# Attention and GELU layer on one core: V of batch 0 issued earlier, loads of batch 2 released earlier and totalled later

## The chip, the cores and the metric

The kernel runs on one core of one Trainium2 chip. The metric is the device time of one execution, in microseconds. The core has five engines that run their own instruction streams in order: TensorE (PE, with its weight loads as PEld), VectorE (DVE), ScalarE (ACT), GpSimd (POOL) and SyncE (SP). DMAs are issued from the queues of SyncE, ScalarE and GpSimd.

## The reference

Batch 8, 12 heads, 448 positions, head size 64. Normalised attention, then a GELU layer over all 3584 tokens:

```python
def rmsnorm(x, g):
    rms = np.sqrt(np.mean(x * x, axis=-1, keepdims=True) + 1e-06)
    return x / rms * g
q_n, k_n = (rmsnorm(q, g_q), rmsnorm(k, g_k))
scores = scale * np.matmul(q_n, k_n.transpose(0, 1, 3, 2))
scores = scores - np.max(scores, axis=-1, keepdims=True)
attn = np.exp(scores)
attn = attn / (np.sum(attn, axis=-1, keepdims=True) + 1e-09)
x = np.matmul(attn, v)            # then (batch, seq, heads * 64)
h = x @ w_in                      # 768 -> 2048
g = 0.5 * h * (1.0 + np.tanh(c * (h + 0.044715 * h * h * h)))
return (g @ w_out)                # 2048 -> 768
```

## The kernel before

**Tiling.** A batch has three groups c of four heads. For each group and each of q and k, one tile of 128 partitions by 896 float32 values is loaded (`load`, L106, 448 KB). It is squared (`square`, L139 on ScalarE, L141 on GpSimd), summed over each head's 64 values (`total`, L146, VectorE), turned into 1/rms (`rsqrt` on ScalarE, L171 to L190, or `rsqrt_newton` on VectorE for batch 1), scaled into bf16 (`normed`, L228) and transposed, either by TensorE (`trans`: `turn` L246, `put` L255 to L259) or by a DMA from SyncE (`dma_trans`, L269). After a DMA transpose `gain` (L275, VectorE) multiplies k by the two gains; it waits for the DMA.

**Attention.** A unit is a group c and one of seven blocks t of 64 keys: eight score matmuls (L288) and one exp on ScalarE (L292) into `ex`. `key_sums` (L308 to L314, VectorE) adds some blocks so that fewer matmuls are needed for the sums. `products(..., 0, ...)` multiplies `ex` with ones (the sums), `products(..., 1, ...)` with V (`vb`), both L336 into the same two PSUM tiles `oall`. So between the two `turned` (L345, VectorE) has to copy the sums away, and `quad_x` (L360, VectorE) has to read the V products before the next group's sums. `recips` is L351 and L352.

**Order.** The whole order is written out by hand (`manual_schedule`): each engine executes in the order in which the program calls it. `first_attention` runs batch 0's 21 units one by one with the lists `side` and `mid` hung on the units. Then for each batch b the loop runs the first matrix product of b (`mm1_pair` L433, `mm1` L369, GELU in L438 and L375) with the list `m1`, and `attention(b + 1, ...)`, which interleaves the second matrix product (`mm2`, L389, copied out by L412, stored by SyncE in L421). `attention` takes two units as a group, i = 0 to 10, and starts each group with the entries of `side` under that number; the sums of c = 0 and 1 stand in groups 4 and 8, their V products and `quad_x` in groups 5 and 9; those of c = 2 come after the last group.

**Loads and buffers.** The tiles of q and of k come from rings of four buffers each. Before any load is issued, buffers are handed out in the order in which the program frees earlier ones. At the start a fourth tile of each is taken and marked by VectorE (`held`, L557), and GpSimd frees it with `released` (L641) after its second w_out load. `late_loads` (L120) does a load after a memset of one element by VectorE, so that SyncE issues the load only when VectorE has come to that place; `loads` has no such memset. Squares that GpSimd makes for batch 2 go into two buffers (`sqp`), so a square waits for the total that reads the one two before it.

**The start.** q of batch 0, group 0 is loaded in two halves, k in a part of four blocks (`t_first`) and a rest of three (`t_rest`). SyncE issues the first of each, ScalarE the second; behind them SyncE issues groups 1 and 2. GpSimd's first instructions are two small loads of the gains (L73), the identity, the square of k's rest (L598), part of q's scaling, two small products (L610, L611), the squares of group 1, then V (`load_v`, L129), the squares of group 2, and the loads of w_in (L576, eight in all) and w_out (L579).

Of the kernel before, what the change touches and what calls it, by code (L numbers as in the profile page):

```python
# [17 lines left out]
def kernel(  # L18
# [11 lines left out]
    nc = tc.nc  # L30
# [11 lines left out]
    HP = H // 2  # L42
# [57 lines left out]
    def load(b, c, n, parts=1, engs=(nc.sync,)):  # L100
        t = rawqk.tile([P, 2, NT, D], F32, tag=f"raw{n}", name=f"raw{n}")
        src = {"q": q, "k": k}[n]
        raws[n, b, c] = t
        m = 2 // parts
        return [
            lambda i=i: engs[i].dma_start(  # L106
                t[:, i * m:(i + 1) * m].rearrange("p a t d -> p a (t d)"),
                src[b, 4 * c + 2 * i * m:4 * c + 2 * (i + 1) * m].rearrange(
                    "(a r) (p t) d -> (r p) a (t d)", r=2, t=NT
                ),  # L110
            )
            for i in range(parts)
        ]

    def loads(b, c):
        for n in "qk":
            for go in load(b, c, n):
                go()

    def late_loads(b, c):  # L120

        for n in "qk":
            for go in load(b, c, n):
                nc.vector.memset(raws[n, b, c][:1, 0, 0, :1], 0.0)
                go()

    def load_v(b, i, n):

        nc.gpsimd.dma_start(  # L129
            vb[b % 2][:, i:i + n].rearrange("p a t d -> p a (t d)"),  # L130
            v[b, 2 * i:2 * (i + n)].rearrange("(a r) (p t) d -> (r p) a (t d)", r=2, t=NT),
        )

    def square(b, c, n, eng, hs=both, ts=slice(0, NT)):
        if (n, b, c) not in sqs:
            sqs[n, b, c] = sqp.tile([P, 2, NT, D], F32, tag="sq", name="sq")
        sq, raw = sqs[n, b, c][:, hs, ts], raws[n, b, c][:, hs, ts]
        if eng is nc.scalar:
            nc.scalar.activation(sq, raw, AF.Square)  # L139
        else:  # L140
            eng.tensor_mul(sq, raw, raw)  # L141

    def total(b, c, n, hs=both, ts=slice(0, NT)):
        if b not in sss:
            sss[b] = smp.tile([P, NCH, 2, 2, NT], F32, tag="ss", name="ss")
        nc.vector.reduce_sum(  # L146
            sss[b][:, c, "qk".index(n), hs, ts], sqs[n, b, c][:, hs, ts], axis=AX.X
        )
# [44 lines left out]
    def rsqrt_newton(b):  # L193

        rinvs[b] = smp.tile([P, NCH, 2, 2, NT], F32, tag="rinv", name="rinv")
        flat = "p c n a t -> p (c n a t)"
        y, ms = rinvs[b].rearrange(flat), sss[b].rearrange(flat)
        t = smp.tile([P, NCH * 4 * NT], F32, tag="lg", name="lg")
        nc.vector.tensor_scalar(ms, ms, 1.0 / D, 1e-6, op0=ALU.mult, op1=ALU.add)
        nc.vector.tensor_scalar(  # L200
            y.bitcast(I32), ms.bitcast(I32), -0.5, float(0x5F3759DF), op0=ALU.mult, op1=ALU.add
        )
        for i in range(3):
            nc.vector.tensor_mul(t, y, y)
            nc.vector.scalar_tensor_tensor(t, t, -0.5, ms, op0=ALU.mult, op1=ALU.mult)
            if i < 2:
                nc.vector.scalar_tensor_tensor(y, t, 1.5, y, op0=ALU.add, op1=ALU.mult)
        m = 4 * NT
        for i, c in enumerate((1, 0, 2)):
            dst = y[:, c * m:(c + 1) * m]  # L210
            if c != 1:
                dst = place(b, c)
            nc.vector.scalar_tensor_tensor(  # L213
                dst, t[:, c * m:(c + 1) * m], 1.5, y[:, c * m:(c + 1) * m],
                op0=ALU.add, op1=ALU.mult,
            )

    def idle(n, w):

        for _ in range(n):  # L220
            nc.tensor.matmul(w, zeros[:, :128], zeros, start=True, stop=True)
# [39 lines left out]
    def trans(b, c):  # L261
        for n in "qk":
            turn(b, c, n)
            put(b, c, n)
# [9 lines left out]
    def gain(b, c):  # L274
        nc.vector.tensor_scalar(kT[:, c], kT[:, c], gcol[:, 0:1], None, op0=ALU.mult)  # L275
# [255 lines left out]
    def plan(*entries):  # L531
        steps = {}
        for slot, *fns in entries:
# [4 lines left out]
    t_first, t_rest = slice(0, 4), slice(4, NT)  # L538
    halves = load(0, 0, "q", 2, (nc.sync, nc.scalar))
    raws["k", 0, 0] = rawqk.tile([P, 2, NT, D], F32, tag="rawk", name="rawk")  # L540
    halves += [
        lambda ts=ts, eng=eng: eng.dma_start(
            raws["k", 0, 0][:, :, ts].rearrange("p a t d -> p a (t d)"),
            k[0, :4].rearrange("(a r) (p t) d -> r p a t d", r=2, t=NT)[:, :, :, ts]
            .rearrange("r p a t d -> (r p) a (t d)"),
        )
        for ts, eng in ((t_first, nc.sync), (t_rest, nc.scalar))
    ]
    for go in halves:
        go()  # L550
# [33 lines left out]
    def warm():  # L584
        return oall[0][:, :S]

    def gpsimd_waits(x):

        nc.gpsimd.tensor_copy(mark, x)  # L589
# [4 lines left out]

    q_only, k_only = slice(0, 1), slice(1, 2)

    idle(18, warm())
    square(0, 0, "k", nc.gpsimd, ts=t_rest)  # L598
    for a in range(2):
# [13 lines left out]
    nc.vector.transpose(gcols, gprod)  # L613
    square(0, 1, "q", nc.gpsimd)
    square(0, 1, "k", nc.gpsimd)
    load_v(0, 0, HP)
    square(0, 2, "q", nc.gpsimd)
    square(0, 2, "k", nc.gpsimd)
    w_in_part(0, 2)
# [19 lines left out]
    def released():  # L639
        for t in held:  # L640
            nc.gpsimd.memset(t[:1, 0, 0, :1], 0.0)  # L641

    side = [(1, lambda: loads(1, 0)),
            (7, lambda: loads(1, 1)),
            (14, lambda: loads(1, 2))]
# [38 lines left out]
    def transposed(b, c):  # L684
        for n in "qk":
            dma_trans(b, c, n)

    def squared(b, c, n, a):
        square(b, c, n, nc.scalar, slice(a, a + 1))

    def normed_both(b, c, eng):
        for n in "qk":
            normed(b, c, n, eng)

    m2 = []
    for b in range(B):
        m1, side = [], []
        if b == 0:

            m1 = [(0, lambda: total(1, 1, "q"),  # L700
                   lambda: total(1, 1, "k"), lambda: total(1, 2, "q"), lambda: total(1, 2, "k"),
                   lambda: rsqrt_newton(1), lambda: normed_both(1, 1, nc.gpsimd)),
                  (4, lambda: transposed(1, 1), lambda: normed_both(1, 0, nc.vector),
                   lambda: normed_both(1, 2, nc.vector)),
                  (5, lambda: trans(1, 0)),
                  (7, lambda: trans(1, 2))]
            side += [(2, lambda: gain(1, 1), lambda: late_loads(2, 0)),
                     (3, lambda: late_loads(2, 1), lambda: late_loads(2, 2))]
            for c, slots in ((0, (4, 5)), (1, (6, 7)), (2, (8, 9))):
                for n, slot in zip("qk", slots):  # L710
                    side += [(3, lambda c=c, n=n: square(2, c, n, nc.gpsimd)),
                             (slot, lambda c=c, n=n: total(2, c, n))]
        elif b + 1 < B:

            m1.append((0, lambda: gpsimd_waits(ess[b, NCH - 1][:1, 0, :1])))
            for c in range(NCH):
                m1 += [(0, lambda c=c: normed_both(b + 1, c, nc.gpsimd)),
                       (4 * c + 4, lambda c=c: transposed(b + 1, c))]
            m1 += [(9, lambda: gain(b + 1, 0)), (14, lambda: gain(b + 1, 1))]
            side.append((3, lambda: gain(b + 1, 2)))  # L720
        if 0 < b and b + 2 < B:
            m1 += [(4, lambda: loads(b + 2, 1)), (8, lambda: loads(b + 2, 2))]
            for c, at in ((0, 4), (1, 9)):
                for i, (n, a) in enumerate((n, a) for n in "qk" for a in range(2)):
                    m1.append((at + i, lambda c=c, n=n, a=a: squared(b + 2, c, n, a)))
                m1 += [(at + 2, lambda c=c: total(b + 2, c, "q")),
                       (at + 4, lambda c=c: total(b + 2, c, "k"))]
            for n in "qk":
                m1.append((13, lambda n=n: square(b + 2, 2, n, nc.gpsimd)))
                side.append((0, lambda n=n: total(b + 2, 2, n)))  # L730
        m1 = plan(*m1)
        for f in range(nf // 2 if b == 0 else nf):
            if b == 0:
                if f > 1:
                    mm1_pair(f)
            elif f in (1, 3):
                mm1_pair(f // 2, late, b)
            elif f > 3:
                mm1(b, f)
            for fn in m1.get(f, ()):  # L740
                fn()
        m2 += m2_parts(b)
        if b + 1 == B:
            for fn in m2:
                fn()
            break
        nc.scalar.preload_act_table_set(EXP_SET)  # L747
        if b + 2 < B:
            side += [(10, lambda: rsqrt(b + 2)),
                     (0 if b else 5, lambda: load_v(b + 2, 0, HP))]  # L750
            if b + 3 < B:
                side.append((1, lambda: loads(b + 3, 0)))
        attention(b + 1, m2, 96 if b == 0 else 112, plan(*side))


# [28 lines left out]
```

## Time and profile before

| | |
|---|---|
| Runs of the kernel before | median 424.75 us (423.63 to 426.59, 3 runs) |
| Profiled execution | 426.47 us, of which the span from first to last instruction is 424.7 us |
| Granted TensorE clock, mean | 0.996 |
| Bytes moved by DMA | 54.06 MB; read 45.61 MB, written 11.01 MB |
| First attention, last exp ends | 33.2 us |
| Attention of batch 1, first scores to first sums of group 2 | 55.5 to 88.5 us |
| Each batch from then on | 48.4 us |

A share of busy time is a mean over the whole span. What a stage is worth is read from the waits in that stage: a line of the timeline has its start, its busy time, engine, line, operation, `out<-in`, and in brackets the idle time of the engine ahead of it with what ended that. In the chain of waits each piece has start, length, and the engine or DMA. A line of the DMA view has the packets of a queue, its MB, and the time of those packets as a share of 16 DMA engines; q0 is GpSimd's queue, q1 SyncE's, q10 ScalarE's.

### The profile page before, as it was taken

To read this page: it belongs to the slowest core of one execution; us is meant where nothing else is said; L and a number is where in the kernel's file an instruction comes from. 1 tells how busy PE (TensorE), PEld (TensorE's weight loads), DVE (VectorE), ACT (ScalarE), POOL (GpSimd) and SP (SyncE) were. 2 spreads that over 40 slices of the span, in tenths; PEclk is the share of its full clock that TensorE was granted. 3 is DMA by queue.
4 is the path that set the end of the run, shared out by engine and by line. 5 is a ranking of instruction groups with operands and counts; after the bars stand their busy time and mean duration, and the time that the engine had idled before them with its cause. 6 is when DMAs were issued, how large, how long until landed. Compare 5 with 4: busy or idle time off the path is not lost.

```text
span 424.7 us, 8042 instructions
## 1 busy us (share of the span) xinstructions
PE 406.5 (96%) x3321; PEld 204.5 (48%) x3321; DVE 259.2 (61%) x433; ACT 274.9 (65%) x365; POOL 124.8 (29%) x103
## 2 busy tenths in 40 slices
PE   6879996999999999999999999999999999999995
PEld 2344553445445554445455444545445454455553
DVE  4979635873589455982589455992579604891010
ACT  4985385638877478748788378847878348754300
POOL 5992304572300840054400930045400800000000
PEclk9999999999999999999999999999999999999999
DMA  8999997489611947239711857139421621120023
GB/s 267 221 240 214 201 226 269 73 150 279 131 39 39 220 122 188 72 82 264 152 39 39 201 141 188 42 87 256 78 60 39 125 45 37 39 65 13 0 76 74
DMA packets 65572, 54.06 MB, mean 127 GB/s; under 512 B 37376, under 2 KB 60544, under 8 KB 65536
## 3 DMA queue, kind: packets, MB, share of 16 engines
q1 hardware_dynamic: 52832, 41.23, 37.2%
q0 software_dynamic: 12128, 11.80, 17.7%
q10 hardware_dynamic: 576, 0.52, 0.4%
q8 instruction: 26, 0.43, 0.4%
q14 instruction: 10, 0.08, 0.1%
HBM read 45.61 MB, written 11.01 MB: 133 GB/s over the span
## 4 chain that ended last, share of the span: by engine, by line
PE 77%; DMA 8%; ACT 6%; DVE 4%; POOL 2%; issue 1%; SPq 0%; DVEq 0%; POOLq 0%
PE o L389 30%; PE h L369 22%; PE o L336 9%; PE hh L433 8%; PE sc L288 7%; ACT ex L292 3%; DMA kT<-nrmk 3%; DMA vb<-in_v_dram 2%; ACT L747 2%; DVE ss L146 1%; DMA rawq<-in_q_dram 1%; DMA rawk<-in_k_dram 1%; DVE st L345 1%; ACT g L375 1%; DVE xT L360 1%
## 5 line engine op out<-in xcount | busy, mean ns | idle before, releaser
L292 ACT ACTIVATE ex<-sc,shift 128x896 bf16<-128x896 f32 x168 | 159.3, 1005 | 36.4 <-PE sc L288 35.7
L389 PE MATMUL o<-wout,g 128*128 128x384 bf16 x896 | 159.8, 328 | 0.0
L389 PEld LDWEIGHTS <-g 128*128 128x128 bf16 x896 | 81.4, 98 | 72.4 <-issue 24.5
L369 PE MATMUL h<-xT,win 128*128 128x448 bf16 x504 | 96.5, 352 | 0.0
L146 DVE TENSOR_REDUCE ss<-sq 128x14 f32<-128x896 f32 (+3 forms) x43 | 44.5, 1038 | 59.6 <-ACT sq L139 52.1
L369 PEld LDWEIGHTS <-win 128*128 128x128 bf16 x504 | 49.3, 98 | 46.0
L412 DVE COPY osb<-o 128x384 f32<-128x384 f32 x51 | 28.1, 550 | 59.6 <-PE o L389 59.4
L375 ACT ACTIVATE g<-h 128x448 bf16<-128x448 f32 x84 | 45.7, 544 | 28.1 <-PE h L369 23.0
L288 PE MATMUL sc<-qT,kT 64*64 64x448 bf16 x672 | 53.1, 365 | 4.3 <-ACT ex L292 2.9
L438 ACT ACTIVATE g<-hh 128x896 bf16<-128x896 f32 x22 | 19.3, 915 | 56.4 <-PE hh L433 56.4
L433 PE MATMUL hh<-xT,win 128*128 128x448 bf16 x264 | 52.9, 353 | 0.3 <-ACT g L438 0.3
L336 PE MATMUL o<-ex,vb 64*64 64x448 bf16 x672 | 38.2, 354 | 4.8 <-DVE st L345 3.2
L589 POOL COPY mark<-es 1x1 bf16<-1x1 bf16 x6 | 1.1, 177 | 139.0 <-DVE es L310 139.0
L228 POOL TENSOR_TENSOR nrmq<-rawq,rinv 128x896 bf16<-128x896 f32 (+1 forms) x21 | 34.7, 1653 | 11.3 <-DVE o L213 10.3
L433 PEld LDWEIGHTS <-win 128*128 128x128 bf16 x264 | 24.6, 98 | 26.1 <-issue 5.0
L288 PEld LDWEIGHTS <-kT 64*64 64x64 bf16 x672 | 16.9, 104 | 36.7 <-issue 33.1
L228 POOL TENSOR_TENSOR nrmk<-rawk,rinv 128x896 bf16<-128x896 f32 x19 | 32.1, 1688 | 0.0
L141 POOL TENSOR_TENSOR sq<-rawq 128x896 f32<-128x896 f32 x9 | 15.1, 1682 | 56.1 <-DVE ss L146 36.1
L345 DVE STREAM_TRANSPOSE st<-o 128x448 f32<-128x448 f32 x46 | 27.0, 625 | 6.5 <-PE o L336 6.4
L360 DVE TENSOR_TENSOR xT<-o,rb 128x448 bf16<-128x448 f32 x48 | 27.6, 617 | 3.4 <-PE o L336 3.2
L336 PEld LDWEIGHTS <-vb 64*64 64x64 bf16 x672 | 19.7, 107 | 19.0 <-issue 7.0
L313 DVE TENSOR_TENSOR e<-ex 128x896 bf16<-128x896 bf16 x38 | 23.3, 612 | 7.0 <-ACT ex L292 7.0
(80 smaller groups left out, 267.5 us busy)
## 6 DMA issues: line engine op xcount, KB each, us to landing
out_dram<-osb SPq DMA_DIRECT2D x54, 192.0 KB, 2.7
rawq<-in_q_dram SPq DMA_DIRECT2D x23, 448.0 KB, 4.3
rawk<-in_k_dram SPq DMA_DIRECT2D x23, 448.0 KB, 5.4
vb<-in_v_dram POOLq DMA_DIRECT2D x8, 672.0 KB, 6.7
win<-in_moe_w_in_dram POOLq DMA_DIRECT2D x8, 384.0 KB, 16.7
wout<-in_moe_w_out_dram POOLq DMA_DIRECT2D x2, 1536.0 KB, 28.5
qT<-nrmq SPq DMA_TRANSPOSE x19, 4.7
kT<-nrmk SPq DMA_TRANSPOSE x19, 4.3
```

Source lines behind the costliest of these rows:

```text
L146: nc.vector.reduce_sum(sss[b][:, c, "qk".index(n), hs, ts], sqs[n, b, c][:, hs, ts], axis=AX.X)
L228: eng.tensor_mul(nrms[n, b, c][:, ts].rearrange("p t a d -> p a t d"), raws[n, b, c][:, :, ts], root[:, :, ts].to_broadcast([P, 2, m, D]),)
L288: nc.tensor.matmul(sc[r * R:(r + 1) * R, a, :S], kT[rs, c, t, r], qT[b][rs, c, :, r], start=True, stop=True,)
L292: nc.scalar.activation(ex[:, t], sc[:, :, :S], AF.Exp, scale=scale, bias=shift)
L336: nc.tensor.matmul(o[r][a * D:(a + 1) * D], vb[b % 2][rs, 2 * c + a, i] if what else ones[rs], es[i][rs, a], start=(i == 0), stop=(i == n ...
L345: nc.vector.transpose(st[:, r].rearrange("p a b -> p (a b)"), oas[0][r])
L360: nc.vector.tensor_mul(xT[b][:, 2 * c + r], oall[r][:, :S], oas["rb"][:, r])
L369: nc.tensor.matmul(h[:, :S], win[:, c, f * 128:(f + 1) * 128], xT[b][:, c], start=(c == 0), stop=(c == HP - 1),)
L375: nc.scalar.activation(g[:, f, (b % 2) * S:(b % 2 + 1) * S], h[:, :S], AF.Gelu_apprx_tanh)
L389: nc.tensor.matmul(o[:, :HD], g[:, f, i * 128:(i + 1) * 128], wout[:, f, half * HD:(half + 1) * HD], start=(f == 0), stop=(f == nf - 1),)
L412: nc.vector.tensor_copy(part, o[:, :HD])
L433: nc.tensor.matmul(h[:, j, :S], win[:, c, f * 128:(f + 1) * 128], xT[b][:, c], start=(c == 0), stop=(c == HP - 1),)
```

## The change

1. The load of k's rest (batch 0, group 0) is issued by SyncE, third on its queue, and no longer by ScalarE.
2. V of batch 0 is issued by GpSimd ahead of its first square; before, it stood between the squares of groups 1 and 2.
3. In the attention of batch 1, group 2, the marked loads of batch 2's c = 0 stand ahead of `gain(1, 1)`. Their totals move: c = 0 from groups 4 and 5 to 5 and 6, c = 1 from 6 and 7 to 7 and 8, c = 2 from 8 and 9 to both in 9.
4. The loads of batch 3's c = 0 move from group 1 of that attention, where they were plain `loads`, to group 7 as `late_loads`. With that the buffers are handed out in another order: batch 2's c = 0 gets the tiles that `released` frees, where before batch 3's c = 0 had them.

TensorE's instructions and their order are the same; VectorE has two memsets more.

```diff
@@ -539,12 +539,12 @@
     halves = load(0, 0, "q", 2, (nc.sync, nc.scalar))
     raws["k", 0, 0] = rawqk.tile([P, 2, NT, D], F32, tag="rawk", name="rawk")
     halves += [
-        lambda ts=ts, eng=eng: eng.dma_start(
+        lambda ts=ts: nc.sync.dma_start(
...
-        for ts, eng in ((t_first, nc.sync), (t_rest, nc.scalar))
+        for ts in (t_first, t_rest)
     ]
@@ -594,6 +594,7 @@
+    load_v(0, 0, HP)
     idle(18, warm())
     square(0, 0, "k", nc.gpsimd, ts=t_rest)
@@ -613,7 +614,6 @@
     square(0, 1, "q", nc.gpsimd)
     square(0, 1, "k", nc.gpsimd)
-    load_v(0, 0, HP)
     square(0, 2, "q", nc.gpsimd)
@@ -704,9 +704,9 @@
-            side += [(2, lambda: gain(1, 1), lambda: late_loads(2, 0)),
+            side += [(2, lambda: late_loads(2, 0), lambda: gain(1, 1)),
                      (3, lambda: late_loads(2, 1), lambda: late_loads(2, 2))]
-            for c, slots in ((0, (4, 5)), (1, (6, 7)), (2, (8, 9))):
+            for c, slots in ((0, (5, 6)), (1, (7, 8)), (2, (9, 9))):
                 for n, slot in zip("qk", slots):
                     side += [(3, lambda c=c, n=n: square(2, c, n, nc.gpsimd)),
                              (slot, lambda c=c, n=n: total(2, c, n))]
@@ -749,7 +749,7 @@
             if b + 3 < B:
-                side.append((1, lambda: loads(b + 3, 0)))
+                side.append((1, lambda: loads(b + 3, 0)) if b else (7, lambda: late_loads(3, 0)))
```

## The prediction

> **What bounds the kernel now.** I read the page first, then the chain of waits in order of time, then the waits of two stretches and their timelines.
>
> ```profile
> span 424.7 us, 8042 instructions
> PE 406.5 (96%) x3321; PEld 204.5 (48%) x3321; DVE 259.2 (61%) x433; ACT 274.9 (65%) x365; POOL 124.8 (29%) x103
> PE 77%; DMA 8%; ACT 6%; DVE 4%; POOL 2%; issue 1%; SPq 0%; DVEq 0%; POOLq 0%
> ```
>
> TensorE sets the end, and from 109 us on it is full: in the table of stretches, 109.0 to 157.4 has 48.07 of 48.40 us busy, and each later batch repeats it. Nothing edited there can bring much; what an early stage gains or loses is carried to the end unchanged. The early stages hold most of the chain's 8% of DMA. Its pieces:
>
> ```profile
> 1.23 4.87 DMA rawk<-in_k_dram
> 12.39 10.32 DMA vb<-in_v_dram
> 48.08 14.29 DMA kT<-nrmk
> 62.90 4.98 DMA rawq<-in_q_dram
> 68.02 1.69 POOL sq L141
> 69.73 1.09 DVE ss L146
> 70.82 1.10 DVE st L345 x2
> ```
>
> The first piece is k of batch 0, group 0 (its first part), the second V of batch 0, the third the transpose that `gain(1, 1)` waits for, the rest q of batch 2. Two of them become idle TensorE, seen in the timeline with the wait in brackets:
>
> ```profile
> 22.75 0.76 PE L336 MATMUL o<-ex,vb 64*64 64x448 bf16 x12 [1.56 <-DMA vb<-in_v_dram]
> 23.76 1.95 ACT L292 ACTIVATE ex<-sc,shift 128x896 bf16<-128x896 f32 x2 [1.51 <-PE sc L288]
> ...
> 69.73 1.09 DVE L146 TENSOR_REDUCE ss<-sq 128x14 f32<-128x896 f32 x1 [4.62 <-POOL sq L141]
> 71.42 0.38 PE L336 MATMUL o<-ex,vb 64*64 64x448 bf16 x2 [3.04 <-DVE st L345]
> ```
>
> In the first attention ScalarE's exps set the pace (13.6 to 33.2 us almost without a gap), and 1.51 us of idle ScalarE is the echo of V. At 67.8 us VectorE, in order, stands at the total of q for batch 2, whose square came late because its load came late, because its marking memset stood behind `gain(1, 1)`; the transposes of the sums (L345) stand behind it, and TensorE behind those. The table of stretches shows what that idleness does next (after PE, PEld, DVE, ACT and POOL comes the granted clock):
>
> ```profile
> 73.00:74.00 1.00, 1.00 (x11) 0.28 (x4) 1.00 (x3) 0.00 (x0) 0.00 (x0) 0.50 0.10 25
> 74.00:75.00 1.00, 1.00 (x7) 0.26 (x10) 1.00 (x2) 0.00 (x0) 0.08 (x1) 0.50 0.00 0
> ```
>
> **The change part by part.**
>
> *Loads of batch 2 ahead of the scaling, totals later.* Group 5's scores start at 67.81, group 6's at 74.70: 6.89 us. Groups 9 and 10, of the same content (V products, two output matmuls), start at 82.92 and 85.18: 2.26. Group 6 to 7 takes 2.57, an ordinary step (60.77 to 62.97) 2.20. So the stall costs 4.63 + 0.37 = 5.0 us: 3.04 + 0.15 of waiting and about 3.5 us (72.6 to 76.1) at half clock, 1.75.
> Is it gone? The two memsets of group 2 (0.06 each) move to before the scaling, at the end of the sum at 59.44 + 0.61 = 60.05, not 62.79. Their tiles are now the ones that GpSimd frees at 34.2, so nothing else holds them. SyncE stood idle for that memset (9.5 us) and issues q 2.8 us sooner. It will not land 2.8 us sooner for certain: the ring still holds the transposes, which land at 62.4, and q of batch 3, next behind them, landed at 63.4, its k at 65.6. I take those two times for q and k. But even at the old 67.9 the total would not stop anyone: it now stands behind L345 and the reciprocal. Without it L345 starts when TensorE's sums end, 66.3; two transposes 1.17, reciprocal 0.33, L352 1.11, copy 0.55: the total runs at 69.6, the first scaling of x (L360) at 70.7 to 71.8, needed by the sums of group 8 at about 74.9.
> What is late next: two square buffers, so each square needs the total two before it. Squares 1.68, totals 1.08: q of group 1 runs 70.7 to 72.4, k 72.9 to 74.6, group 2's end by 76.3 and 78.0; the totals wait about 0.1 us in all. The price comes at the end: both totals of group 2 now stand between L352 and the last sums, 1.08 us more and 0.12 of added memsets. There L310 ends at 87.90 and TensorE wants it at 88.52: 0.62 of cover, so 0.5 to 0.8 is lost; I take 0.6. The rsqrt on ScalarE waits about 1 us too; its last exp still ends before those sums. Net 4.4.
> *Loads of batch 3 from group 1 to group 7.* Two loads leave SyncE's place at 51.43 (there behind the transposes, so these gain nothing) for about 73, behind two memsets. Output stores are next on that queue at 79.39. The squares want the data at 97.1; a load there takes 5 to 7 us. Cost nothing, cover 17 us.
> *V first on GpSimd.* Issuing it takes 0.91 us in the 2.45 that GpSimd waits for k's rest (idle 3.19 to 5.64); it gives 0.9 back at 12.39. V needed 10.3 us at 12.4 and is wanted at 21.2; from 3.2 it has 18. The wait of 1.56 goes; what ScalarE had idle, 1.5, is the gain. The DVE product wanted next at 23.4 is just in time.
> What it meets: q and k of groups 1 and 2 (landed 7.3, 8.8, 10.0, 11.1), 1792 B packets on SyncE's ring at some 235 a us. Group 1's k is wanted by its square at 10.77, and ScalarE's rsqrt behind has no slack. How the two queues share:
>
> ```profile
> q0 software_dynamic: 143, 0.27, 71.8%
> q1 hardware_dynamic: 139, 0.25, 37.4%
> ```
>
> That is 26 to 28 us, GpSimd's queue first: packet for packet. V needs 2 us from issue to its first packets (12.39 to 14.4), longer behind the small g loads, whose last packets came near 7. If V starts at 7, k has 270 packets to go at 110 a us: it lands at 10.1, no loss. From 5.3 it lands at 10.6 to 10.9. Lower bound 0, upper bound the load of k of batch 1, which beside V took 12.4 us where 4.2 was usual: 4.8 late. I take 0.5, near the packet count. The Trainium skill (DMA: Bandwidth & Descriptors, Queues, rings and completion order) says that an engine takes turns between queues by whole packets of several descriptors. These rows agree on turns, and from 16 to 18 us V's queue moved 419 packets and SyncE's none. By turns that long the term would be near 4.8 and the sum 1.5, on the way to the slower rival below.
> *k's rest on SyncE.* ScalarE loses a 0.46 us issue in a wait; SyncE's four later loads go 0.5 later, still 3 us or more ahead of their data. k's first part no longer shares with the rest: both together moved 0.46 MB between 4.0 and 6.1, so the first part should land near 5.2 and the rest near 6.0, not 6.1 and 5.64. The chain starts at that first part, at most 0.9 early; GpSimd's square of the rest, then its q product (7.27), hold it to 0.3 to 0.5. If V presses the rest back, up to 0.6 is lost. I take +0.4.
>
> **Sum:** 4.4 + 1.5 + 0.4 - 0.5 = 5.8. The profiled execution took 426.47 (span 424.7, 1.8 around it); 426.5 - 5.8 = 420.7. It lies 1.7 above the median of the runs, 424.75, so I state 419.0.
>
> The clock part rests on one place. The Trainium skill (TensorE: Matmul & The Clock Gate, What's actually happening) gives an idle window of about 3.4 us before the clock halves. Here 3.04 us of waiting was enough. By its figure the halved clock would not belong to this stall, which is the fourth rival.
>
> **Rivals.**
> *The first stage gains nothing.* w_in, w_out and the transposes keep the DMA engines full until 62; the second half of w_out landed at 66.7 (33.0 + 33.7), and its first user, the 49th output matmul, ran near 67.7. Or group 1's k lands 1.9 late. Against it: V leaves that queue by 14 instead of 20, and the engines had a quarter free from 11 to 15, which should bring w_out some 1.5 us. Then 4.4 is left: 420.4.
> *The stall moves.* The totals of group 2 stand ahead of the second L360, two copies and the last sums; if the squares of group 2 come 2 to 3 us late, TensorE waits there. For it: GpSimd waited 10.0 us for totals in this stretch. Against it: by the schedule above the squares are 1.2 to 2.9 ahead. Price about 3.3, so a gain of 2.5: 422.2.
> *Slower.* V's burst holds SyncE's ring as it did from 16 to 18. If k of group 1 pays all of the 8.2 us (12.4 against 4.2) that k of batch 1 paid, it lands at 17.4, its square starts 6.7 later than now, ScalarE stands, and 6.7 - 1.5 - 4.4 leaves 0.8: 425.6. It decides from a landing 5.9 us past the need; a late q or k of group 2 behind it would take it to 430. Against it: these loads are issued before V.
> *The half clock stays*, as something other than this stall brings it. Against it: the clock is 1.00 in every stretch before and in all of a later batch. The stall is then worth 1.75 less, the gain is 4.0: 420.7.
> *The earlier release does nothing*, because the ring holds q back. The totals' new place suffices: same time.
>
> **How the numbers follow.** About 1% (4.25 us) is what a measurement of this kernel tells from no change. Forecast, a gain of 4.5 to 7: 0.40. More than 7: 0.05. No first-stage gain: 0.20, half of it over 4.25. Stall moved: 0.20. Half clock stays: 0.05. Slower: 0.10, of which 0.06 beyond 1%. Faster 0.40 + 0.05 + 0.10 = 0.55, slower 0.06, same 0.39. The range leaves out the slower case and the far gain: 416.8 to 424.4; the likeliest alone is 417.7 to 420.3.
>
> **What would show it.** Right: no TensorE wait for vb near 21; no wait over 1 us for L345 near 66; clock 1.00 throughout the second attention; group 5 to 6 in about 2.3 us; k's first square before 5.6. Wrong: ScalarE idle before the rsqrt of group 1, TensorE waiting on w_out near 65, or on L360 or L310 near 83.

## The result and the profile after

| | before | after |
|---|---|---|
| Median of 12 runs each, side by side | 424.77 us (422.72 to 426.97) | 420.09 us (419.46 to 423.58) |
| Profiled execution | 426.47 us, span 424.7 | 419.69 us, span 417.9 |
| First attention's last exp done (the table load that follows it starts) | 33.22 us | 30.98 us |
| Attention of batch 1 begins (table load L747) | 55.80 us | 53.67 us |
| The same place one batch on | 109.70 us | 102.85 us |
| From there to the end | 315.0 us | 315.0 us |

The ratio is 0.990, 95% interval [0.987, 0.993]: a gain of 4.7 us, 1.1%. The span of the profiled execution lost more, 6.8 us: 2.1 before the attention of batch 1 and 4.7 in the 54 us behind that point (53.90 became 49.18). The last row is the same, so the explanation lies in the first 110 us.

The page after, the lines for the span, the engines and the chain's shares:

```profile
span 417.9 us, 8046 instructions
PE 405.1 (97%) x3321; PEld 205.0 (49%) x3321; DVE 259.9 (62%) x435; ACT 274.7 (66%) x365; POOL 125.1 (30%) x103
PE 84%; ACT 9%; DVE 3%; POOL 2%; issue 1%; POOLq 0%; ACTq 0%
```

DMA had 8% of the chain and is gone from it. TensorE's busy time fell by 1.4 us of the 6.8, about what the matmuls at half clock had taken longer; the rest was idleness. The timeline of the same kernel at the places of the prediction (brackets: idle time ahead and what ended it):

```profile
5.01 0.61 ACT L139 ACTIVATE sq<-rawk 128x512 f32<-128x512 f32 x1
...
5.82 0.82 POOL L141 TENSOR_TENSOR sq<-rawk 128x384 f32<-128x384 f32 x1 [1.82 <-DMA rawk<-in_k_dram]
...
12.93 0.32 ACT L171 ACTIVATE lg<-ss,eps 128x28 f32<-128x28 f32 x1 [0.32 <-DVE ss L146]
...
20.36 0.74 PE L336 MATMUL o<-ex,vb 64*64 64x448 bf16 x12
...
64.21 1.18 DVE L345 STREAM_TRANSPOSE st<-o 128x448 f32<-128x448 f32 x2 [0.97 <-PE o L336]
...
65.68 0.57 PE L288 MATMUL sc<-qT,kT 64*64 64x448 bf16 x8
...
66.08 1.49 PE L336 MATMUL o<-ex,vb 64*64 64x448 bf16 x28
...
67.94 0.57 PE L288 MATMUL sc<-qT,kT 64*64 64x448 bf16 x8
...
78.86 0.36 ACT L171 ACTIVATE lg<-ss,eps 128x84 f32<-128x84 f32 x1 [1.02 <-DVE ss L146]
...
81.67 0.38 PE L336 MATMUL o<-es,ones 64*64 64x448 bf16 x4 [0.50 <-DVE es L310]
```

The V products at 20.36 and 66.08 carry no bracket: neither V nor L345 is waited for. VectorE now stands idle for TensorE at L345 (0.97), where before TensorE stood for VectorE. Group 5 to group 6 is 67.94 - 65.68 = 2.26 us. The last two lines show the price: the rsqrt waits 1.02 for the last totals, the last sums 0.50 for L310. The table of stretches of the same kernel (after the engines the granted clock, DMA share, GB/s):

```profile
73.00:74.00 1.00, 1.00 (x25) 0.51 (x14) 1.00 (x2) 1.00 (x2) 1.00 (x2) 1.00 0.81 294
74.00:75.00 1.00, 1.00 (x7) 0.61 (x8) 1.00 (x3) 0.39 (x1) 1.00 (x1) 1.00 1.02 333
```

Full clock, where before it was 0.50. The mean clock of this profile is 0.997 all the same: the last matmul ends at 413.47 us, and behind it, from 415.48 us on, the clock halves at no cost.

### The profile page after: what moved, and what is told of

The parts are those of the page before. It is cut to its first block, busy times and chain, and to the rows that moved or that the text cites. A ratio compares the mean times of both kernels' runs of the same rounds, so it can differ in the third digit from the quotient of the medians.

```text
span 417.9 us, 8046 instructions
## 1 busy us (share of the span) xinstructions
PE 405.1 (97%) x3321; PEld 205.0 (49%) x3321; DVE 259.9 (62%) x435; ACT 274.7 (66%) x365; POOL 125.1 (30%) x103
## 4 chain that ended last, share of the span: by engine, by line
PE 84%; ACT 9%; DVE 3%; POOL 2%; issue 1%; POOLq 0%; ACTq 0%
PE o L389 31%; PE h L369 23%; PE hh L433 12%; PE o L336 9%; PE sc L288 8%; ACT ex L292 6%; ACT L747 2%; DVE ss L146 1%; PE tp L246 1%; POOL g L141 1%; ACT g L375 1%; DVE st L345 0%; DVE rb L352 0%; POOL grow L73 0%; POOL nrmq L228 0%
## 5 line engine op out<-in xcount | busy, mean ns | idle before, releaser
L336 PE MATMUL o<-ex,vb 64*64 64x448 bf16 x672 | 37.3, 350 | 0.0
L345 DVE STREAM_TRANSPOSE st<-o 128x448 f32<-128x448 f32 x46 | 27.0, 625 | 6.9 <-PE o L336 6.9
L352 DVE STREAM_TRANSPOSE rb<-rc 128x896 f32<-128x896 f32 x24 | 26.7, 1112 | 0.8
```

The lines of the kernel that those rows point to most:

```text
L336: nc.tensor.matmul(o[r][a * D:(a + 1) * D], vb[b % 2][rs, 2 * c + a, i] if what else ones[rs], es[i][rs, a], start=(i == 0), stop=(i == n ...
L345: nc.vector.transpose(st[:, r].rearrange("p a b -> p (a b)"), oas[0][r])
```

## The experiments

Three sets, each on one chip beside the kernel before. Its medians there: 425.88 us (35 runs), 425.40 (21), 426.22 (11). The theory: the batch 2 edits bring most of the gain by ending one stall and the half clock behind it, V early brings the rest, and k's rest brings little. Rivals: V and k's rest bring nothing by themselves; one of the two batch 2 edits does nothing; and, for the gap between 6.8 and 4.7 us, that the profiled execution of before was only one of several kinds.

### First set: the parts alone

**control**: the kernel before, unchanged.

> The kernel before, unchanged, to see how its runs spread. Theory one (every execution has the 3 us stall near 68 us and TensorE at half clock for some 3.5 us behind it): mean granted clock 0.996 in all runs, and a spread of times below 1 us. Theory two (the stall is in every execution, but whether and how long the clock halves behind it differs from execution to execution): the runs' clock goes from about 0.992 to 1.000, and the time falls as the clock rises, some 1.7 us for each 0.004. Median 424.8 us either way.

Measured: 426.13 us (423.77 to 428.27, 12 runs), ratio 1.0021 [0.9992, 1.005]. Its profiled execution lost its time elsewhere than the one shown before the change. The timeline of control:

```profile
22.69 0.76 PE L336 MATMUL o<-ex,vb 64*64 64x448 bf16 x12 [2.04 <-DMA vb<-in_v_dram]
...
71.02 0.32 PE L389 MATMUL o<-wout,g 128*128 128x384 bf16 x1 [1.74 <-DMA wout<-in_moe_w_out_dram]
...
73.25 0.38 PE L336 MATMUL o<-ex,vb 64*64 64x448 bf16 x2 [1.41 <-DVE st L345]
```

and its stretches behind the first of these waits:

```profile
24.00:25.00 1.00, 1.00 (x16) 0.55 (x12) 0.00 (x0) 0.87 (x1) 1.00 (x1) 0.50 1.17 187
25.00:26.00 1.00, 1.00 (x12) 0.38 (x5) 0.00 (x0) 0.27 (x1) 1.00 (x2) 0.50 1.13 224
```

Here the half clock stands behind V (2.04 us of idle TensorE), and the wait for L345 is 1.41, not 3.04, since TensorE had already stood 1.74 for w_out. So the stall and the half clock that I costed are not fixed properties of the kernel before; an execution has one, the other, or more.

**start_only**: items 1 and 2 of the change, none of batch 2's.

```diff
-        lambda ts=ts, eng=eng: eng.dma_start(
+        lambda ts=ts: nc.sync.dma_start(
...
+    load_v(0, 0, HP)
     idle(18, warm())
...
-    load_v(0, 0, HP)
     square(0, 2, "q", nc.gpsimd)
```

> Only the edits of the start: V of batch 0 issued ahead of GpSimd's first square, and k's rest by SyncE; the attention of batch 1 as in the kernel before. If the start's gain is carried through to the end (theory: exps of the first attention end 2.2 us earlier, and each stage behind them by as much): 422.6 us. If the stages up to 62 us are set by the DMA engines (w_in, w_out, transposes), the gain is gone by group 3 of the second attention: 424.5 us, with TensorE waiting there for wout or kT.

Measured: 422.73 us (421.38 to 428.15, 12 runs; 422.36 without the longest), ratio 0.9944 [0.9915, 0.9974].

**v_only**: V early alone.

```diff
+    load_v(0, 0, HP)
     idle(18, warm())
...
-    load_v(0, 0, HP)
     square(0, 2, "q", nc.gpsimd)
```

> Only V of batch 0 moved ahead of GpSimd's first square; k's rest stays on ScalarE's queue. Theory (the wait for V was worth 1.5 us, and V's burst comes after the q and k loads): 423.3 us, first exp at 10.9 us as before, no wait for vb. Rival (V's packets take turns with q and k of group 1 and hold ScalarE's rsqrt back): 424.3 to 425.5 us, with GpSimd waiting for the load of k of group 1 before its square at 10.8 us.

Measured: 422.11 us (421.21 to 425.74, 12 runs), ratio 0.9947 [0.9916, 0.9979]. With k's rest on SyncE as well the time is not lower. Neither kernel waits for V. Both keep the stall of batch 2, and they happen to show two gaps of nearly the same length that end differently. The timeline of start_only and its stretches, then of v_only the same:

```profile
68.30 0.38 PE L336 MATMUL o<-ex,vb 64*64 64x448 bf16 x2 [2.29 <-DVE st L345]
68.83 2.29 PE L336 MATMUL o<-ex,vb 64*64 64x448 bf16 x26 [0.15 <-DVE st L345]
```

```profile
70.00:71.00 1.00, 1.00 (x12) 0.23 (x2) 1.00 (x3) 0.00 (x0) 0.00 (x0) 0.50 0.11 29
71.00:72.00 1.00, 1.00 (x8) 0.32 (x10) 1.00 (x2) 0.00 (x0) 0.21 (x1) 0.50 0.00 0
```

```profile
68.62 0.38 PE L336 MATMUL o<-ex,vb 64*64 64x448 bf16 x2 [2.20 <-DVE st L345]
69.15 1.51 PE L336 MATMUL o<-ex,vb 64*64 64x448 bf16 x26 [0.16 <-DVE st L345]
```

```profile
70.00:71.00 1.00, 1.00 (x16) 0.30 (x8) 1.00 (x3) 0.00 (x0) 0.17 (x1) 1.00 0.16 47
```

Nearly the same gap (2.29 and 2.20); behind the one the 26 matmuls took 2.29 us at half clock, behind the other 1.51. The last section comes back to this.

**batch2_only**: items 3 and 4, none of the start.

```diff
-            side += [(2, lambda: gain(1, 1), lambda: late_loads(2, 0)),
+            side += [(2, lambda: late_loads(2, 0), lambda: gain(1, 1)),
...
-            for c, slots in ((0, (4, 5)), (1, (6, 7)), (2, (8, 9))):
+            for c, slots in ((0, (5, 6)), (1, (7, 8)), (2, (9, 9))):
...
-                side.append((1, lambda: loads(b + 3, 0)))
+                side.append((1, lambda: loads(b + 3, 0)) if b else (7, lambda: late_loads(3, 0)))
```

> Only the edits in the attention of batch 1: loads of batch 2 ahead of the scaling, totals one to two groups later, loads of batch 3 in group 7. V of batch 0 and k's rest as in the kernel before. If the stall at 68 us and its half clock go in all runs (the prediction's term of 4.4 us): 420.4 us. If the half clock is there in only some of the runs of the kernel before, only the wait of 3.2 us less 0.6 goes in the middle run: 422.2 us. If the later totals move the stall behind the reciprocals of group 8: 422 to 424 us, and TensorE waiting over 2 us near 85 us. In the profile: no wait for L345 near 68 us, and a wait of about 0.5 us for L310 near 84.

Measured: 419.85 us (419.27 to 424.4, 12 runs), ratio 0.9895 [0.9857, 0.9934]. No wait for L345 and full clock in the second attention; TensorE waited 1.08 us for V, and 4 of the 12 runs lie above 421.5 us. The timeline of batch2_only:

```profile
21.92 0.76 PE L336 MATMUL o<-ex,vb 64*64 64x448 bf16 x12 [1.08 <-DMA vb<-in_v_dram]
```

Here the batch 2 edits alone reached the time of the whole change (ratios 0.9895 and 0.990).

### Second set: which part of the start counts

**after_again**: the changed kernel once more.

> The changed kernel again, beside the next three on one chip. Theory one (the start's gain is real and carried to the end: V is early, and TensorE never idles long enough in the first attention for its clock to halve): about 2 us below batch2_again, 419.5 to 420.5 us. Theory two (with the stall of the second attention gone, the start sets nothing in the middle run, because V lands in time often enough or the stages up to 62 us wait for DMA): within 0.5 us of batch2_again.

Measured: 420.57 us (420.0 to 423.64, 6 runs), ratio 0.9891 [0.9852, 0.9931]. The profiled execution was the longest of them, and shows why. Its timeline and its stretches:

```profile
7.99 0.82 POOL L141 TENSOR_TENSOR sq<-rawk 128x384 f32<-128x384 f32 x1 [3.98 <-DMA rawk<-in_k_dram]
...
9.87 0.56 PE L246 MATMUL tp<-ident,nrmq 128*128 128x128 bf16 x7 [3.45 <-POOL nrmq L228]
```

```profile
12.00:13.00 1.00, 1.00 (x10) 0.21 (x6) 1.00 (x2) 0.94 (x1) 1.00 (x2) 0.50 1.23 226
13.00:14.00 1.00, 1.00 (x9) 0.45 (x5) 0.55 (x2) 0.62 (x2) 1.00 (x2) 0.50 1.14 319
```

k's rest, third on SyncE's queue, landed 6.2 us after its issue instead of 4.0. GpSimd's square of it began at 7.99 instead of 5.82, its scaling of q and so TensorE's first transposes followed, and the 3.45 us gap brought a half-clock stretch. V did not press the load back: from 3 to 7 us GpSimd's queue moved only 64 packets, together less than 0.01 MB.

**batch2_again**: batch2_only once more, on this chip.

> Only the edits in the attention of batch 1, once more, beside the changed kernel. Theory one: 421.5 to 422.5 us, with a wait for vb of 1 to 2 us in its trace and now and then the clock halved behind it. Theory two: the time of after_again within 0.5 us, though its trace still shows the wait for vb.

Measured: 421.88 us (419.28 to 424.74, 10 runs), ratio 0.9905 [0.9872, 0.9938]. V was waited for 1.76 us, and w_in, issued behind V by GpSimd, as well:

```profile
22.15 0.76 PE L336 MATMUL o<-ex,vb 64*64 64x448 bf16 x12 [1.76 <-DMA vb<-in_v_dram]
...
35.76 4.51 PE L433 MATMUL hh<-xT,win 128*128 128x448 bf16 x23 [0.75 <-DMA win<-in_moe_w_in_dram]
```

**v_batch2**: the changed kernel, with k's rest left on ScalarE.

```diff
-        lambda ts=ts: nc.sync.dma_start(
+        lambda ts=ts, eng=eng: eng.dma_start(
...
-        for ts in (t_first, t_rest)
+        for ts, eng in ((t_first, nc.sync), (t_rest, nc.scalar))
```

> The changed kernel but for k's rest, which stays on ScalarE's queue. If SyncE's order for k is worth its 0.4 us of the prediction (or the 0.66 by which GpSimd's first scaling came earlier in the traces): 0.4 to 0.7 us above after_again. If the first part of k lands early or late by chance (it landed early in the trace of the unchanged control too): the same time as after_again within 0.5 us, first exp anywhere from 9.8 to 10.9 us.

Measured: 419.90 us (419.32 to 420.23, 5 runs, all at a mean clock of 1.0), ratio 0.9863 [0.9822, 0.9904]. Without item 1 nothing is lost: the time is 0.67 us under after_again, which neither theory had. One wait is longer than in the profile after. The timeline of v_batch2:

```profile
61.76 1.68 POOL L141 TENSOR_TENSOR sq<-rawq 128x896 f32<-128x896 f32 x1 [16.16 <-DVE es L314]
62.07 1.85 DVE L310 TENSOR_TENSOR es<-es,ex 128x896 bf16<-128x896 bf16 x1
...
63.98 0.38 PE L336 MATMUL o<-es,ones 64*64 64x448 bf16 x4 [0.69 <-DVE rawk L124]
```

q of batch 2 landed early, so GpSimd's square ran at the same time as VectorE's add L310. The add, 0.61 us where no square runs beside it, took 1.85, and the sums waited 0.69 us.

**k_batch2**: the changed kernel, with V in its old place.

```diff
-    load_v(0, 0, HP)
     idle(18, warm())
...
+    load_v(0, 0, HP)
     square(0, 2, "q", nc.gpsimd)
```

> The edits in the attention of batch 1 and k's rest by SyncE, but V of batch 0 where it was. If the start's gain is V's (theory one): 1.5 us above after_again, 421 to 422 us, with a wait for vb of 1 to 2 us near 21. If it is k's: the time of after_again. A shorter way to the first exp cannot shorten the wait for V by itself, as V then is issued 0.7 us earlier too.

Measured: 422.25 us (420.92 to 424.42, 12 runs), ratio 0.9922 [0.9899, 0.9945]. The time is that of the first theory, but the wait is not: the profile shows none for V and 1.06 us for w_in:

```profile
35.30 4.51 PE L433 MATMUL hh<-xT,win 128*128 128x448 bf16 x23 [1.06 <-DMA win<-in_moe_w_in_dram]
```

On this chip V early is worth 1.7 to 2.0 us by the medians (k_batch2 against after_again, batch2_again against v_batch2). k's rest by SyncE goes with 0.4 and 0.7 us more (batch2_again against k_batch2, v_batch2 against after_again). The intervals of the ratios overlap in all four pairs. For V the single runs support the medians: 5 of the 6 of after_again lie below the fastest of the 12 of k_batch2. For k's rest a small loss is likely but not shown, and no gain is seen.

### Third set: which of the batch 2 edits, and the price at the end

**v_totals**: V early; of batch 2 only the totals' new places.

```diff
-            side += [(2, lambda: late_loads(2, 0), lambda: gain(1, 1)),
+            side += [(2, lambda: gain(1, 1), lambda: late_loads(2, 0)),
...
-                side.append((1, lambda: loads(b + 3, 0)) if b else (7, lambda: late_loads(3, 0)))
+                side.append((1, lambda: loads(b + 3, 0)))
```

(against v_batch2, as the next two.)

> V early and the totals of batch 2 one to two groups on; batch 2's marked loads stay behind the scaling of k and batch 3's first loads stay in group 1. If the totals' new place suffices, as the prediction's last rival has it: no wait over 1 us for L345 near 66, full clock there, and the same time as v_batch2_again, about 419.9; perhaps 0.5 less, since GpSimd's square of q comes later than L310 and no longer runs beside it (0.61 us for that add, not 1.85). If the earlier release is needed too: VectorE stands at the first total near 67 to 69, the scaling of x or the sums of a later group wait 1 us or more, and the time is 421 to 422.

Measured: 419.91 us (419.33 to 421.7, 6 runs), ratio 0.9845 [0.9811, 0.9879]. The timeline of v_totals:

```profile
66.19 1.68 POOL L141 TENSOR_TENSOR sq<-rawq 128x896 f32<-128x896 f32 x1 [20.10 <-DMA rawq<-in_q_dram]
...
67.90 1.09 DVE L146 TENSOR_REDUCE ss<-sq 128x14 f32<-128x896 f32 x1 [0.39 <-POOL sq L141]
...
82.33 0.38 PE L336 MATMUL o<-es,ones 64*64 64x448 bf16 x4 [0.97 <-DVE es L310]
```

The square begins at 66.19, and the total waits 0.39 for it, but behind L345 nobody notices until the last sums: 0.97 us for L310 instead of 0.5.

**v_release**: V early; the earlier release, the totals in their old places.

```diff
-            for c, slots in ((0, (5, 6)), (1, (7, 8)), (2, (9, 9))):
+            for c, slots in ((0, (4, 5)), (1, (6, 7)), (2, (8, 9))):
```

> V early and the earlier release of batch 2's loads (with batch 3's moved to group 7), the totals in their old groups 4 to 9. If the earlier release alone suffices: the square of q ends by about 64, the total of group 4 waits for nothing, TensorE waits under 1 us for L345 near 66, and the time is that of v_batch2_again, about 419.9, also without the wait of about 0.5 ahead of the last sums. If the total still blocks the transposes of the sums: a TensorE wait of 1 to 3 us for L345, perhaps with a half-clock stretch behind it, and 421 to 423.

Measured: 420.41 us (419.61 to 421.22, 6 runs), ratio 0.9853 [0.9817, 0.9889]. The timeline of v_release:

```profile
62.18 1.64 DVE L310 TENSOR_TENSOR es<-es,ex 128x896 bf16<-128x896 bf16 x1
63.81 1.09 DVE L146 TENSOR_REDUCE ss<-sq 128x14 f32<-128x896 f32 x1
...
63.87 0.38 PE L336 MATMUL o<-es,ones 64*64 64x448 bf16 x4 [0.55 <-DVE rawk L124]
...
64.81 1.18 DVE L345 STREAM_TRANSPOSE st<-o 128x448 f32<-128x448 f32 x2
...
66.54 1.49 PE L336 MATMUL o<-ex,vb 64*64 64x448 bf16 x28
```

The total still stands ahead of L345, but it no longer waits; the V products at 66.54 have no bracket. Compared with the totals in their new places (0.50 to 0.51 us for L310 at the end, in the profile after and in v_batch2_again) the price has only moved: 0.55 us at the first sums, where the add ran beside the square, and none for L310 at the end.

**v_last_total**: v_batch2 with the last total one group later and ScalarE's rsqrt behind the last exp.

```diff
-            for c, slots in ((0, (5, 6)), (1, (7, 8)), (2, (9, 9))):
+            for c, slots in ((0, (5, 6)), (1, (7, 8)), (2, (9, 10))):
...
-            side += [(10, lambda: rsqrt(b + 2)),
+            side += [(10 if b else 11, lambda: rsqrt(b + 2)),
```

and in `attention`, ahead of the GELU's table load: `for fn in side.get(len(groups), ()): fn()`.

> As v_batch2, with the last total of batch 2 (k of group 2) one group later, behind L310, and ScalarE's rsqrt behind the last exp. If the totals ahead of L310 are what TensorE's wait of 0.5 at the last sums and the rsqrt's wait of 1.02 pay for: both waits go, and the time is 0.4 to 0.6 under v_batch2_again, about 419.4. Rival: the later rsqrt makes GpSimd's scalings and the transposes of batch 2 late, and nothing or less than nothing comes of it: 419.9 or above.

Measured: 419.82 us (419.15 to 420.32, 5 runs), ratio 0.9836 [0.9801, 0.9872]. Two timelines, first v_last_total, then v_batch2_again:

```profile
79.81 0.62 DVE L310 TENSOR_TENSOR es<-es,ex 128x896 bf16<-128x896 bf16 x1
80.34 1.08 DVE L146 TENSOR_REDUCE ss<-sq 128x14 f32<-128x896 f32 x1
...
80.89 0.38 PE L336 MATMUL o<-es,ones 64*64 64x448 bf16 x4
...
82.26 1.17 DVE L345 STREAM_TRANSPOSE st<-o 128x448 f32<-128x448 f32 x2
...
102.35 1.28 ACT L749 ACT_TABLE_LOAD   x1
```

```profile
80.81 0.62 DVE L310 TENSOR_TENSOR es<-es,ex 128x896 bf16<-128x896 bf16 x1
...
81.47 0.38 PE L336 MATMUL o<-es,ones 64*64 64x448 bf16 x4 [0.51 <-DVE es L310]
...
82.27 1.18 DVE L345 STREAM_TRANSPOSE st<-o 128x448 f32<-128x448 f32 x2
...
102.66 1.28 ACT L747 ACT_TABLE_LOAD   x1
```

The wait for L310 is gone and the sums start 0.58 earlier, but the total now stands ahead of the next transposes, which start at 82.26 as before. By the next table load 0.31 us is left, and the medians, 0.17 apart, do not resolve it.

**v_batch2_again**: v_batch2 once more, beside these three.

> V early and all edits of batch 2, k's rest by ScalarE as in the kernel before: the reference of the other three on the same chip. As in its first run about 419.9, all runs near full granted clock, no half-clock stretch before the last matmul. If the half-clock stretches come at random however short TensorE's gaps are, some of its runs lie 2 to 4 us above that.

Measured: 419.99 us (419.53 to 422.0, 6 runs, 5 of them at a mean clock of 0.998 or more), ratio 0.985 [0.9815, 0.9885]. No wait over 0.55 us in TensorE's second attention, and full clock. One run at 0.996 took 422.0, so a stretch at half clock can still come.

## Why the prediction was right, and where it was not

The predicted 419.0 us is 1.1 below the measured 420.09, within the range and on the right side of 1% (4.7 of 424.8 us). Point by point:

**Batch 2, +4.4: right.** Group 5 to 6 fell from 6.89 to 2.26 us and 6 to 7 from 2.57 to 1.91, less 0.50 at L310 (forecast 0.5 to 0.8). That makes 4.8; the stage shows 4.7. q landed for its square at 64.31 (I had taken 63.4), with room to spare. The half-clock stretch, which I read as 3.5 us and 1.75 us of loss, is 3.41 us and 1.7 by its edges. The rival that the earlier release does nothing because the totals' new place suffices is right in its second half: in v_totals the new place suffices. But v_release shows that the release suffices too. The two edits do the same thing twice, and each alone (with V early) comes to the time of both within what these runs resolve (419.91 and 420.41 against 419.99).

**V early, +1.5, and its contention, -0.5.** The wait for V is gone, as forecast. The contention was mis-sized: in the profile after, GpSimd's squares of group 1 (8.46 and 10.10) wait for no load, and the rsqrt of group 1 runs at 12.93 and waits only 0.32 for its total. V itself took 13.3 us from issue to landing instead of 10.3, which nobody waited for. The slower rival, with a burst that holds SyncE's ring, appears in none of the profiles. Turns as long as V's burst, which I had weighed at up to 4.8 us, did not come: from 8 to 9 us V's queue moved 87 packets and SyncE's 129. The stretch on which I had based them (16 to 18 us before, 419 packets against none) does not show such a turn either, as SyncE issued its next load only at 15.33 us. The term is 0. The rival that the first stage gains nothing fits the first set, where batch2_only is at the time of the whole change, and not the second, where V early is worth 1.7 to 2.0 us. No profile of a kernel with the batch 2 edits has TensorE wait for w_out in the second attention, as that rival would have it.

**k's rest, +0.4: not shown.** In the profile after, k's first part was squared at 5.01 instead of 6.12 and the first exp ran at 9.81 instead of 10.87, of which 0.66 us was left at the rsqrt of group 1. But control, without the edit, had its first exp at 9.82, and k_batch2, with it, at 10.57: so how the loads happen to land moves it as much as the edit. GpSimd's square of k's rest begins at 5.45 to 7.99 us in the four profiles with that load on SyncE, and at 5.12 to 6.05 in the ten with it on ScalarE. The loss that I bounded at 0.6, with V as its cause, was 2.17 us for the square in after_again (7.99 against 5.82); V was not the cause, and the gap behind it brought a half-clock stretch.

**From the profiled execution to the median, 1.7: the step that failed.** I summed the waits of one execution, 5.8 us, and then also took off the 1.7 by which that execution exceeded the median. But the excess was of the same kind as what I had just removed. The span did lose 6.8 us (the sum was 1.0 short), from an execution in which the stall was long and the clock halved; an execution like control's has less to lose there and more elsewhere. The runs of the kernel before in the three sets, and the 18 of the changed kernel, by mean granted clock:

| mean granted clock | before, 67 runs | after, 18 runs |
|---|---|---|
| 0.997 and more | 423.33 us (7 runs) | 420.09 us (14) |
| 0.994 to 0.996 | 425.18 us (33) | the 4 others, 0.992 to 0.996: 423.34 us |
| 0.990 to 0.992 | 426.69 us (25) | |
| below | 428.6 us (2) | |

One stretch of 3.4 us at half clock costs 1.7 us, which is 0.004 of the mean. So the rows stand roughly for none, one, two and three stretches; what the half clock behind the last matmul takes off the mean (0.003 in the profile after) costs no time. The medians of the rows before lie 1.5 to 1.9 us apart. The profiled execution, at 0.996, belongs to the second row. In the top row the two kernels are 3.2 us apart; the rest of the difference of the medians of these runs (425.74 and 420.34) is that 60 of 67 runs before, and only 4 of 18 after, fall below 0.997. So the number of stretches differs from execution to execution; each gap of TensorE of some 2 us or more can bring one, and the change takes away most of these gaps. The clock part of the sum, 1.75 for the one place at 72.6, had the right size for one stretch, but stood for a varying number of them.

**The parts do not add by their medians.** Against 425.9, V alone gave 3.8 us, the batch 2 edits alone 6.0, and v_batch2 against its own 425.4 gave 5.5. By the ratios that is not shown: 0.9947 and 0.9895 multiply to 0.984, which lies inside the interval of v_batch2. With the batch 2 edits made, the best runs with and without V early are alike (419.15 and 419.27). What V early changes is how many runs are long: of 22 runs without it 10 lie above 421.5 us, of 28 with it 2, all with k's rest on ScalarE. With k's rest on SyncE it is 11 of 12 without V early (k_batch2) and 4 of 18 with it (the changed kernel). This count goes across chips, and what the kernels without V early waited for is read only from their three profiles (V 1.08 us; V 1.76 with w_in 0.75; w_in 1.06). Why V comes late in some executions and not in others stays open.

## What to carry to other kernels

Before summing waits from one profiled execution, look whether it is one of several kinds: profile the same kernel twice, and set the times of all runs against their mean granted clock. If the waits sit in different places, size each term for the typical run, and do not take the distance to the median off a second time. An in-order engine that stands ahead of TensorE's needs can be cured by fetching its data earlier or by asking for it later; try each alone, since the second may add nothing but its price at the end.

## What the runs showed of the hardware

TensorE's clock halved behind gaps of 2.04, 2.29, 3.04 and 3.45 us, but not behind 1.08, 1.76 or 2.20. The half clock lasted 3.41 us each of the four times. The Trainium skill (TensorE: Matmul & The Clock Gate, What's actually happening) gives a free-running window of about 3.4 us. The duration agrees; a whole idle window was not needed here.

The traces show the free-running part too. The four profiles with a half-clock stretch (before, control, start_only, after_again) have the clock halved once more behind the last matmul. From the end of the stretch to that second halving it is 348.16, 399.36, 348.16 and 406.19 us. These are 102, 117, 102 and 119 times 3.4133 us, to within 0.01 us. So the halvings and the ends of the stretches lie a whole number of such windows apart, whatever TensorE did in between. I count the windows back from the halving behind the last matmul and read, behind each window, its length and TensorE's busy time; the granted clock is the third number from the end. First start_only, then v_only:

```profile
65.99:69.40 3.41, 0.96 (x19) 0.54 (x18) 2.73 (x5) 1.78 (x2) 3.41 (x3) 1.00 1.00 363
```

```profile
63.93:67.34 3.41, 2.49 (x29) 1.05 (x18) 0.41 (x1) 2.39 (x4) 2.13 (x2) 1.00 1.04 387
67.34:70.75 3.41, 1.97 (x29) 1.07 (x29) 3.34 (x6) 0.85 (x1) 2.83 (x2) 1.00 0.81 293
```

The gap of 2.29 us lies in one window, with 2.45 us idle in all, and the clock halved at its end. The gap of 2.20 is cut in two, 0.92 and 1.44 us idle, and the clock stayed. Ahead of the last matmul, in all 14 profiles, every window with at least 1.85 us of idle TensorE was followed by a half clock, and none with 1.74 or less. Among the windows in which the last matmul ends, one with 2.01 us was (after) and two with 1.81 and 1.99 were not (v_batch2_again, control), so the limit is not sharp.

A VectorE add beside a GpSimd square took 1.85 us instead of 0.61. In v_batch2 the square ended at 61.76 + 1.68 = 63.44 and the add at 63.92, so most of its work came after the square's end: 0.48 of the usual 0.61 us. The Trainium skill (SBUF — State Buffer, SBUF: two separate sides) says that a VectorE instruction with two inputs in SBUF and a GpSimd one that reads SBUF share a pair of ports as an exclusive lock for a whole instruction: whoever starts second stands still. The row agrees with its 0.48 us behind the square's end, and so do after_again (0.48) and v_release (0.49). An earlier load can thus cost time, by setting a GpSimd instruction beside a VectorE one on the path.
